# Score products of batches 1 to 3 on 128 rows throughout, and weighted sums with their 128-column products first

## The chip, the cores and the metric

The kernel runs on one core of one Trainium2 chip. The core has TensorE (PE in the profile; PEld is its weight load), VectorE (DVE), ScalarE (ACT), GpSimd (POOL) and SyncE (SP), each with its own instruction queue that is worked in order, and DMA queues that are fed from SP and ACT. The metric is the device time of one execution in microseconds, as the median of several runs.

## The reference

Attention with rotary positions, 4 batches of 8 heads, 576 positions, head size 64, followed by a two-layer MLP on all 2304 tokens. Everything is float32 on the outside.

```python
def rotate(x):
    x1, x2 = (x[..., :half], x[..., half:])
    return np.concatenate([x1 * cos - x2 * sin, x1 * sin + x2 * cos], axis=-1)
q_rot, k_rot = (rotate(q), rotate(k))
scores = scale * np.matmul(q_rot, k_rot.transpose(0, 1, 3, 2))
scores = scores - np.max(scores, axis=-1, keepdims=True)
attn = np.exp(scores)
attn = attn / (np.sum(attn, axis=-1, keepdims=True) + 1e-09)
x = np.matmul(attn, v)            # then (batch * position, 8 * 64)

h = x @ w_in                      # 512 -> 2048
sp = np.where(h > 20.0, h, np.log1p(np.exp(np.minimum(h, 20.0))))
out = (h * np.tanh(sp)) @ w_out   # 2048 -> 512
```

## The kernel before

The kernel works on pairs of heads: `P` counts 16 of them, four for each batch. A pair's positions are cut into four tiles of 128 queries for each head and one tail tile that holds the last 64 queries of both heads. Every such tile is one step: score products on TensorE into a PSUM tile `psc` (two buffers), maximum on VectorE (L520), exponential with its sum on ScalarE (L522), the reciprocal, and then the weights as a high and a low float16 part `ew` (L536 or L538 for the high one, L542 on VectorE for the low one). A DMA transposes `ew` into `et`. `av` makes the weighted sums: for each pair two of them, over 256 and 320 queries, into the PSUM tile `po`.

To keep accuracy, numbers are split into a high part that TensorE's fast float32 form holds exactly and a low rest. In batch 0 (`P < NP`) a score product is three passes over 64 rows. In batches 1 to 3 a product for one head is two passes, each of two matmuls of 288 columns (L495):

- the first has 128 rows. Its weights `xa` (or `xb` for the second head) hold the high part of q in the rows of the head and q's low part in the other 64 rows; the moving operand `y[:, h]` holds the high part of k twice;
- the second has only the head's own 64 rows: the high part of q times `kl`, the low part of k. `kl` has 128 rows, 64 for each head of the pair.

The tail product of a pair (`scores_tail`) has three passes, all of 128 rows: the two heads' high parts and, for the low part, `xdiag`, which holds the two heads' tail columns of q as a block diagonal, times `kl`. `xdiag` is filled by two copies on ScalarE for each pair (L412).

`kl` is made in `prep_k` by one subtraction on GpSimd with 128 rows and 576 columns (L437), from the rotated k (`raw`, L379 to L382 on GpSimd) and its high part. The high part is copied into `y` by four DMAs (L446). The tile `raw` of k is free for the next pair's load (L373, mostly issued from ScalarE's queue) when the subtraction and those copies are done.

A weighted sum of batches 1 to 3 has three passes: V high with weights high, V low with weights high, V high with weights low. A pass is one matmul with 128 weight columns (L666, the chunk that holds the end of both heads) and four pairs of matmuls with 64 weight columns (L669 and L670, one head each). The three passes are planned as two operations, of two passes and of one.

All other TensorE work is the MLP: L912 makes hidden columns into `ph`, L943 makes the output into `pp` or `po`, always in groups of 12 matmuls with 128 rows and 128 columns. The MLP of one batch is spread among the attention steps of the next.

The order of all this is not written by hand. `Plan.op` records every operation with the engines that may do it and a cost in ns. `Plan.order` plays them through with these costs and priorities and so decides the order of issue on each engine; the costs are hand-set (a score product has 2n x 228 ns for n passes, a weighted sum 17.4 matmul costs). On the chip every engine follows its order strictly.

Of the kernel before, what the change touches and what calls it, by code (L numbers as in the profile page):

```python
# [10 lines left out]
F32 = mybir.dt.float32  # L11
# [258 lines left out]
def attention_mish_mlp(ctx: ExitStack, tc: tile.TileContext, qk, v, vflat, rope, ident_in, w_in, w_out, outT):  # L270
# [14 lines left out]
    def sbuf(shape, dt, tag, bufs=1):  # L285
        return plan.tile(sb, shape, dt, tag, bufs)
# [15 lines left out]
    xq = [fixed((128, 1408), F32R, f"xq{r}") for r in range(2)]  # L302
    for t in (cs, ident, ones, cells, w1, w2, *xt, *xq):
        t()
# [91 lines left out]
    def prep_q(P):  # L396
# [4 lines left out]
        def view(a):  # L401
# [6 lines left out]
           w=parts(o, LO), r=parts(o, HI) + (parts(t, LO) if first else []))  # L408
        for x, p, k in ((xdiag[P % 2], 1, HI), (xlow[P % 2], 0, LO))[:2 if first else 1]:
            for h, a in ((0, 512), (1, 0)):  # L410
                d = slice(64 * h, 64 * h + 64)
                op((ACT, act_ns(64), lambda d=d, a=a, x=x, p=p: nc.scalar.activation(  # L412
                    x()[d, d], view(p)[d, a:a + 64], AF.Copy)), w=[(x, h)], r=parts(o, k))
# [15 lines left out]
    def prep_k(P):  # L429
        t = rope_turn(P, 1)  # L430
        y = sbuf((128, 2, S), F32R, "y", 2)
        first = P < NP
        hi = y if first else t
        kl = y if first else sbuf((128, S), F32R, "kl", 2)

        def low(e):
            e.tensor_tensor(out=kl()[:, 0] if first else kl(), in0=t()[:, 0], in1=hi()[:, 1], op=ALU.subtract)  # L437

        op((ACT, act_ns(S), lambda: nc.scalar.activation(
            hi()[:, 1] if first else hi()[:, 1].bitcast(F32R), t()[:, 0], AF.Copy)), w=parts(hi, HI), r=parts(t, LO))  # L440
        st["K", P] = y, kl
        if not first:
            for h in range(2):
                own = slice(64 * h, 64 * h + 64)
                for r in range(2):
                    load("xy", dma_ns(64 * S * 4, 625), lambda dma, h=h, r=r, own=own: dma(  # L446
                        y()[64 * r:64 * r + 64, h].bitcast(F32), t()[own, 1]), w=[(y, (h, r))], r=parts(t, HI))
        op([(POOL, pool_ns(S), lambda: low(nc.gpsimd)), (DVE, dve_ns(S), lambda: low(nc.vector))][:2 if first else KLW],
           w=parts(kl, LO) if first else [kl], r=parts(hi, HI) + parts(t, LO))

# [20 lines left out]
    def scores(pt, P, h, t):  # L471
        own = slice(64 * h, 64 * h + 64)
        y, kl = st["K", P]
        if P < NP:
            Q = xqs[P]
            q = slice(128 * t + 64 * h, 128 * t + 64 * h + 128)
            need = parts(Q, HI + LO) + parts(y, HI + LO)

            def terms():
                return [(Q()[own, i, q], y()[own, j]) for i, j in ((1, 1), (0, 1), (1, 0))]  # L480
        else:
            x = (xa, xb)[h][P % 2]
            q = slice(128 * (t + h), 128 * (t + h) + 128)
            need = [(x, k) for k in range(3)] + [(y, (h, 0)), (y, (h, 1)), kl]

            def terms():
                return [(x()[:, q], y()[:, h]), (x()[own, q], kl()[own])]

        product(pt, need, terms, 3 if P < NP else 2)

    def product(pt, need, terms, n):
# [4 lines left out]

        op((PE, 2 * n * 228, fn), w=[pt], r=need)

    def scores_tail(pt, P):
        d = xdiag[P % 2]  # L500
        y, kl = st["K", P]
        if P < NP:
            low = xlow[P % 2]
            need = [(low, 0), (low, 1)] + parts(y, HI + LO)

            def terms():
                return [(d(), y()[:, 1]), (low(), y()[:, 1]), (d(), y()[:, 0])]
        else:
            a, b = xa[P % 2], xb[P % 2]
            need = [(z, k) for z in (a, b) for k in range(3)] + [(y, (h, r)) for h in range(2) for r in range(2)] + [kl]  # L510

            def terms():
                return [(a()[:, 512:640], y()[:, 0]), (b()[:, 0:128], y()[:, 1]), (d(), kl())]

        product(pt, need + [(d, 0), (d, 1)], terms, 3)

# [131 lines left out]
    def av(P, k):  # L648
# [13 lines left out]

        def fn(passes):
            for vi, ei in passes:
                et = ET()[:, 9 * ei:9 * ei + 9]
                nc.tensor.matmul(po()[:, :n], V()[:, vi, 4, :], et[:, 4, :], start=vi == 0 and ei == 0, stop=False)  # L666
                for c in range(4):
                    last = ei == 1 and c == 3
                    nc.tensor.matmul(po()[0:64, :n], V()[:, vi, c, 0:64], et[:, c, :], start=False, stop=last)  # L669
# [5 lines left out]
        else:  # L675
            op((PE, 5.8 * pe_ns(2, n), lambda: fn([(0, 0), (1, 0)])), w=[po], r=[(V, 0), (V, 1)] + [(ET, x) for x in need])
            op((PE, 5.8 * pe_ns(1, n), lambda: fn([(0, 1)])), w=[po], r=[(V, 0)] + [(ET, x) for x in need])
        if p == 0 and k == 0:
# [357 lines left out]
    for t in xq:  # L1036
        nc.vector.memset(t()[:, 1152:1408].bitcast(F32), 0.0)
    program()
    with tc.manual_schedule():
# [62 lines left out]
```

## Time and profile before

| | us |
|---|---|
| median of 3 runs | 772.73 |
| lowest and highest run | 768.99 and 781.5 |
| span of the profiled execution, first to last instruction (its own time is not listed apart) | 760.5 |
| PE busy | 676.6 (89% of the span) |
| PEld busy | 493.0 (65%) |
| DVE busy | 484.8 (64%) |
| ACT busy | 401.8 (53%) |
| POOL busy | 304.9 (40%) |

The profile is one execution on the chip. It lists for each engine and line how long the instructions ran, and what ended the idle time before them (the releaser). "Issue" as a releaser means that the profile shows nothing that the engine waited for. Matmuls are pipelined, so what one costs is read from the distance between starts in the timeline rather than from its duration. A form like "64*128 64x288" means weights of 64 rows and 128 columns, and a moving operand of 64 rows and 288 columns. PEclk is the clock that TensorE was granted, as a share of 2.4 GHz.

### The profile page before, as it was taken

To read this page: it belongs to the slowest core of one execution; us is meant where nothing else is said; L and a number is where in the kernel's file an instruction comes from. 1 tells how busy PE (TensorE), PEld (TensorE's weight loads), DVE (VectorE), ACT (ScalarE), POOL (GpSimd) and SP (SyncE) were. 2 spreads that over 40 slices of the span, in tenths; PEclk is the share of its full clock that TensorE was granted. 3 is DMA by queue.
4 is the path that set the end of the run, shared out by engine and by line. 5 is a ranking of instruction groups with operands and counts; after the bars stand their busy time and mean duration, and the time that the engine had idled before them with its cause. 6 is when DMAs were issued, how large, how long until landed. Compare 5 with 4: busy or idle time off the path is not lost. (4 is left out here: it accounts for less than half of the span.)

```text
span 760.5 us, 12953 instructions
## 1 busy us (share of the span) xinstructions
PE 676.6 (89%) x4904; PEld 493.0 (65%) x4904; DVE 484.8 (64%) x873; ACT 401.8 (53%) x828; POOL 304.9 (40%) x268
## 2 busy tenths in 40 slices
PE   1968689786899889997899879988999999999998
PEld 1646566554675557765676567655777776777776
DVE  6899999879768857756367666737466637120110
ACT  3766667666565555645455446625554655242331
POOL 4488865649624736226333653335513101000000
PEclk9966868895999989998999999996999999999999
DMA  9942526266726991497728770766346605300000
GB/s 365 371 135 77 170 80 170 90 157 154 192 51 134 236 225 49 111 173 173 183 50 219 168 174 13 165 172 155 102 87 154 134 1 118 64 9 16 9 9 31
DMA packets 167213, 97.83 MB, mean 129 GB/s; under 512 B 130800, under 2 KB 151408, under 8 KB 167024
## 3 DMA queue, kind: packets, MB, share of 16 engines
q1 hardware_dynamic: 152784, 71.26, 39.3%
q10 hardware_dynamic: 14368, 25.76, 11.1%
q8 instruction: 38, 0.62, 0.3%
q14 instruction: 23, 0.19, 0.1%
HBM read 46.27 MB, written 4.72 MB: 67 GB/s over the span
## 5 line engine op out<-in xcount | busy, mean ns | idle before, releaser
L912 PE MATMUL ph<-xt,w 128*128 128x288 f16 x1344 | 178.9, 292 | 14.3 <-ACT mh L917 14.1
L912 PEld LDWEIGHTS <-w 128*128 128x128 f16 x1536 | 152.0, 100 | 58.8 <-issue 18.0
L943 PE MATMUL pp<-g,w 128*128 128x288 f16 x1344 | 184.3, 291 | 1.1 <-ACT ot L951 1.1
L943 PEld LDWEIGHTS <-w 128*128 128x128 f16 x1536 | 147.1, 99 | 49.0 <-issue 11.5
L522 ACT ACTIVATE e<-psc,mx 128x576 f32<-128x576 f32 x144 | 105.8, 737 | 83.3 <-DVE mx L520 75.7
L495 PE MATMUL psc<-y,xq 128*128 128x288 f32 (+1 forms) x456 | 109.7, 365 | 40.4 <-ACT e L522 25.4
L536 POOL TENSOR_SCALAR ew<-e,rs 128x576 f16<-128x576 f32 x62 | 48.7, 788 | 188.4 <-DVE rs L532 121.9
L542 DVE SCALAR_TENSOR_TENSOR ew<-e,rs,ew 128x576 f16<-128x576 f32 x108 | 106.1, 1009 | 28.4 <-POOL ew L536 16.0
L379 POOL TENSOR_TENSOR raw<-raw,cs 128x576 f32<-128x576 f32 x62 | 98.0, 1596 | 59.4 <-DMA raw<-in_qk 39.6
L929 DVE SCALAR_TENSOR_TENSOR g<-mh,cells,g 128x576 f16<-128x576 f32 x64 | 61.4, 961 | 90.0 <-ACT g L926 89.5
L520 DVE TENSOR_REDUCE mx<-psc 128x1 f32<-128x576 f32 x144 | 106.6, 747 | 18.3 <-PE psc L495 17.5
L495 PEld LDWEIGHTS psc<-y,xq 128*128 128x128 f32 (+1 forms) x456 | 75.1, 221 | 60.7 <-ACT e L522 31.3
L917 ACT ACTIVATE mh<-ph,cells 128x288 f32<-128x288 f32 x112 | 54.6, 497 | 86.3 <-PE ph L912 72.6
L382 POOL TENSOR_TENSOR raw<-raw 128x288 f32<-128x288 f32 x60 | 64.0, 1084 | 0.0
L495 PE MATMUL psc<-kl,xq 64*128 64x288 f32 (+1 forms) x216 | 58.6, 353 | 0.0
L758 POOL TENSOR_TENSOR w<-mr,w 128x512 f16<-128x512 f32 x32 | 41.1, 1291 | 36.9 <-ACT w L756 24.8
L669 PE MATMUL po<-et,v 128*64 128x256 f16 (+1 forms) x288 | 51.9, 306 | 0.0
L670 PE MATMUL po<-et,v 128*64 128x256 f16 (+1 forms) x288 | 51.8, 305 | 0.0
L538 ACT ACTIVATE ew<-e,rs 128x576 f16<-128x576 f32 x46 | 35.3, 771 | 25.6 <-DMA et<-ew 9.8
L495 PEld LDWEIGHTS psc<-kl,xq 64*128 64x128 f32 (+1 forms) x216 | 34.1, 196 | 16.4 <-issue 16.0
L927 DVE TENSOR_SCALAR g<-mh,cells 128x576 f16<-128x576 f32 x21 | 15.5, 738 | 43.6 <-ACT mh L917 22.8
L530 DVE TENSOR_SCALAR sm<-sm 128x2 f32<-128x2 f32 (+1 forms) x80 | 26.9, 336 | 22.2 <-ACT e L522 21.8
(111 smaller groups left out, 809.7 us busy)
## 6 DMA issues: line engine op xcount, KB each, us to landing
raw<-in_qk ACTq DMA_DIRECT2D x22, 576.0 KB, 4.9
xq<-raw SPq DMA_DIRECT2D x48, 144.0 KB, 2.7
y<-raw SPq DMA_DIRECT2D x48, 144.0 KB, 3.6
raw<-in_qk SPq DMA_DIRECT2D x10, 576.0 KB, 4.6
out_dram<-ot ACTq DMA_DIRECT2D x32, 144.0 KB, 1.9
g<-in_w_in SPq DMA_DIRECT2D x4, 1024.0 KB, 7.6
w<-in_w_in SPq DMA_DIRECT2D x4, 1024.0 KB, 15.2
stg<-in_v ACTq DMA_DIRECT2D x11, 320.0 KB, 3.8
```

The lines of the kernel that those rows point to most:

```text
L379: e.tensor_tensor(out=t()[:, :, s], in0=t()[:, :, s], in1=cs()[:, :, s], op=ALU.mult)
L382: e.tensor_tensor(out=t()[:, 0, s], in0=t()[:, 0, s], in1=t()[:, 1, s], op=ALU.add)
L495: nc.tensor.matmul(pt()[:, c, :HS], x, z[:, c * HS:(c + 1) * HS], start=a == 0, stop=a == n - 1)
L520: op((DVE, dve_ns(S), lambda: nc.vector.tensor_reduce(m(), pt()[:, :, :HS], axis=AX.XY, op=ALU.max, negate=True)), w=[m], r=[pt])
L522: op((ACT, act_ns(S, psum=True, ptr=2), lambda: nc.scalar.activation(e().rearrange("p (c s) -> p c s", c=2), pt()[:, :, :HS], AF.Exp, bias ...
L542: op((DVE, dve_ns(S) + 61, lambda: nc.vector.scalar_tensor_tensor(out=w()[:, c], in0=e(), scalar=r()[:, h:h + 1], in1=w()[:, hc], op0=ALU. ...
L669: nc.tensor.matmul(po()[0:64, :n], V()[:, vi, c, 0:64], et[:, c, :], start=False, stop=last)
L670: nc.tensor.matmul(po()[64:128, :n], V()[:, vi, c, 64:128], et[:, 5 + c, :], start=False, stop=last)
L912: nc.tensor.matmul(hp(), w1()[:, wi, cc, f:f + 128], x()[:, xi, cc, hf * HS:(hf + 1) * HS], start=cc == 0 and a == 0, stop=cc == NCC - 1 a ...
L917: op((ACT, act_ns(HS, psum=True, ptr=1), lambda j=j, hp=hp: nc.scalar.activation(hn()[:, j], hp(), AF.Mish, scale=uh())), w=[(hn, j)], r=[ ...
L929: op((DVE, dve_ns(S) + 61, lambda: nc.vector.scalar_tensor_tensor(out=g()[:, 1, f], in0=hn(), scalar=f32(gs), in1=g()[:, 0, f], op0=ALU.mu ...
L943: nc.tensor.matmul(pp()[:, :HS], w2e[e]()[:, wi, f], g()[:, gi, f % 8, :], start=f == 0 and a == 0, stop=f == NF - 1 and a == 2)
```

## The change

Four things are changed.

1. The low part of k is kept in two fixed tiles `klz` of 128 rows, two heads and 576 columns. They are set to zero once at the start, on GpSimd. For each pair, GpSimd writes the low part of head h into the 64 rows of that head only, in two subtractions of 64 rows instead of one of 128. A score product's second pass then uses all 128 rows of q's tile and of `kl[:, h]`; the rows of q's low part meet zeros.
2. The tail has four passes, the high and the low part of k for each head. `xdiag` is no longer used in batches 1 to 3 and its two copies are left out there.
3. A weighted sum is one planned operation; its three 128-column matmuls come first, then the 24 matmuls with 64 columns.
4. The costs for the planner follow: 2n x 132 ns for a score product, in batch 0 too, and 15 matmul costs plus 220 ns for a weighted sum. The scratch memory for DMAs is set to 1024 bytes.

```diff
+    klz = [fixed((128, 2, S), F32R, f"kl{r}", planned=False) for r in range(2)]
...
-        for x, p, k in ((xdiag[P % 2], 1, HI), (xlow[P % 2], 0, LO))[:2 if first else 1]:
+        for x, p, k in ((xdiag[P % 2], 1, HI), (xlow[P % 2], 0, LO))[:2 if first else 0]:
...
-        kl = y if first else sbuf((128, S), F32R, "kl", 2)
-
-        def low(e):
-            e.tensor_tensor(out=kl()[:, 0] if first else kl(), in0=t()[:, 0], in1=hi()[:, 1], op=ALU.subtract)
+        kl = y if first else klz[P % 2]
+
+        def low(e, rows=slice(0, 128), h=0):
+            e.tensor_tensor(out=kl()[rows, h], in0=t()[rows, 0], in1=hi()[rows, 1], op=ALU.subtract)
...
+        for h in range(0 if first else 2):
+            rows = slice(64 * h, 64 * h + 64)
+            op([(POOL, pool_ns(S), lambda rows=rows, h=h: low(nc.gpsimd, rows, h)),
+                (DVE, dve_ns(S), lambda rows=rows, h=h: low(nc.vector, rows, h))][:KLW],
+               w=[(kl, h)], r=parts(hi, HI) + parts(t, LO))
...
-                return [(x()[:, q], y()[:, h]), (x()[own, q], kl()[own])]
+                return [(x()[:, q], y()[:, h]), (x()[:, q], kl()[:, h])]
...
-        op((PE, 2 * n * 228, fn), w=[pt], r=need)
+        op((PE, 2 * n * 132, fn), w=[pt], r=need)
...
-                return [(a()[:, 512:640], y()[:, 0]), (b()[:, 0:128], y()[:, 1]), (d(), kl())]
-
-        product(pt, need + [(d, 0), (d, 1)], terms, 3)
+                ends = a()[:, 512:640], b()[:, 0:128]
+                return [(ends[h], z[:, h]) for z in (y(), kl()) for h in range(2)]
+
+        product(pt, need, terms, 3 if P < NP else 4)
...
-        def fn(passes):
-            for vi, ei in passes:
-                et = ET()[:, 9 * ei:9 * ei + 9]
-                nc.tensor.matmul(po()[:, :n], V()[:, vi, 4, :], et[:, 4, :], start=vi == 0 and ei == 0, stop=False)
+        def fn():
+            passes = [(vi, ET()[:, 9 * ei:9 * ei + 9]) for vi, ei in ((0, 0), (1, 0), (0, 1))]
+            for i, (vi, et) in enumerate(passes):
+                nc.tensor.matmul(po()[:, :n], V()[:, vi, 4, :], et[:, 4, :], start=i == 0, stop=False)
+            for i, (vi, et) in enumerate(passes):
                 for c in range(4):
...
-            op((PE, 5.8 * pe_ns(2, n), lambda: fn([(0, 0), (1, 0)])), w=[po], r=[(V, 0), (V, 1)] + [(ET, x) for x in need])
-            op((PE, 5.8 * pe_ns(1, n), lambda: fn([(0, 1)])), w=[po], r=[(V, 0)] + [(ET, x) for x in need])
+            op((PE, 5 * pe_ns(3, n) + 220, fn), w=[po], r=[(V, 0), (V, 1)] + [(ET, x) for x in need])
...
+    for t in klz:
+        nc.gpsimd.memset(t().bitcast(F32), 0.0)
```

## Rows read from the trace of the kernel before

**Rows 1.** Windows: stretch, then busy us of each engine (instructions), clock, DMA.

```profile
156.00:280.00 124.00, 105.10 (x696) 71.91 (x697) 99.39 (x170) 70.81 (x148) 70.46 (x56) 0.88 0.71 166
280.00:521.00 241.00, 221.56 (x1683) 159.09 (x1680) 153.00 (x258) 124.20 (x251) 100.27 (x86) 0.98 0.59 138
521.00:645.00 124.00, 123.88 (x931) 90.64 (x932) 74.38 (x126) 70.68 (x140) 30.68 (x31) 0.96 0.49 109
```

**Rows 2.** Waits of PE from 280 to 521 us: total us, times, longest.

```profile
PE psc L495 <- ACT e L522: 8.8, 3, 5.0
PE ph L912 <- ACT mh L917: 8.4, 7, 2.0
```

**Rows 3.** The chain that ended last: start us, us, what.

```profile
497.75 0.77 DVE mx L520
...
521.12 3.04 PE psc L495 x10
...
528.27 19.48 PE ph L912 x144
...
600.40 17.66 PE ph L912 x144
```

**Rows 4.** Timeline of PE: start us, us, instruction, tile, form, count.

```profile
402.14 0.31 PE L666 MATMUL po<-et,v 128*128 128x320 f16 x1
402.38 0.32 PE L669 MATMUL po<-et,v 128*64 128x320 f16 x1
...
402.81 0.30 PE L669 MATMUL po<-et,v 128*64 128x320 f16 x1
...
403.05 0.53 PE L495 MATMUL psc<-y,xq 128*128 128x288 f32 x2
403.51 0.53 PE L495 MATMUL psc<-kl,xq 64*128 64x288 f32 x2
403.97 1.64 PE L943 MATMUL pp<-g,w 128*128 128x288 f16 x12
405.36 0.78 PE L495 MATMUL psc<-y,xq 128*128 128x288 f32 x4
405.98 0.42 PE L495 MATMUL psc<-kl,xq 128*128 128x288 f32 x2
406.24 1.64 PE L943 MATMUL pp<-g,w 128*128 128x288 f16 x12
```

**Rows 5.** Groups by line and form: busy us, mean ns, idle before and releasers.

```profile
L495 PEld LDWEIGHTS psc<-kl,xq 64*128 64x128 f32 x192 | 29.7, 194 | 16.4 <-issue 16.0 <-POOL kl L437 0.2 <-POOL raw L379 0.2
```

**Rows 6.** Three lines' own views: duration in ns (min/median/max), first and last start.

```profile
L437 POOL TENSOR_TENSOR kl<-raw x12: 1400/1411/2008, 124.8 to 574.4; 128x576 fp32r<-128x576 f32 x12
L412 ACT ACTIVATE xq<-raw x24: 239/252/257, 125.2 to 575.2; 64x64 fp32r<-64x64 f32 x24
L542 DVE SCALAR_TENSOR_TENSOR ew<-e,rs,ew x108: 799/818/2009, 162.2 to 647.7; 128x576 f16<-128x576 f32 x108
```

**Rows 7.** Timeline of all engines from 439 to 452 us.

```profile
439.12 1.95 DVE L542 SCALAR_TENSOR_TENSOR ew<-e,rs,ew 128x576 f16<-128x576 f32 x1
...
440.42 1.92 POOL L437 TENSOR_TENSOR kl<-raw 128x576 fp32r<-128x576 f32 x1
...
450.80 0.33 ACTq L373 DMA_DIRECT2D raw<-in_qk  x1
...
451.74 1.51 PE L912 MATMUL ph<-xt,w 128*128 128x288 f16 x11 [1.96 <-ACT mh L917]
```

**Rows 8.** Timeline of the start: GpSimd's first rotation.

```profile
6.08 3.54 POOL L379 TENSOR_TENSOR raw<-raw,cs 128x576 f32<-128x576 f32 x2 [5.64 <-DMA raw<-in_qk]
```

**Rows 9.** Groups by form, 156 to 280 us, then 280 to 521 us.

```profile
L495 PE MATMUL psc<-kl,xq 64*128 64x288 f32 x48 | 13.3, 359 | 0.0
L495 PE MATMUL psc<-kl,xq 64*128 64x288 f32 x94 | 25.8, 355 | 0.0
```

**Rows 10.** Windows, as rows 1: behind the chain's part without TensorE.

```profile
515.00:532.00 17.00, 15.10 (x67) 9.66 (x68) 13.84 (x18) 9.53 (x19) 8.99 (x8) 0.61 0.61 144
```

More of the change, by code (lines that the diff above doesn't have):

```diff
@@ L302, in attention_mish_mlp @@
     xq = [fixed((128, 1408), F32R, f"xq{r}") for r in range(2)]
-    for t in (cs, ident, ones, cells, w1, w2, *xt, *xq):
+    klz = [fixed((128, 2, S), F32R, f"kl{r}", planned=False) for r in range(2)]
+    for t in (cs, ident, ones, cells, w1, w2, *xt, *xq, *klz):
         t()
@@ L447, in prep_k @@
                         y()[64 * r:64 * r + 64, h].bitcast(F32), t()[own, 1]), w=[(y, (h, r))], r=parts(t, HI))
-        op([(POOL, pool_ns(S), lambda: low(nc.gpsimd)), (DVE, dve_ns(S), lambda: low(nc.vector))][:2 if first else KLW],
-           w=parts(kl, LO) if first else [kl], r=parts(hi, HI) + parts(t, LO))
+        if first:
+            op([(POOL, pool_ns(S), lambda: low(nc.gpsimd)), (DVE, dve_ns(S), lambda: low(nc.vector))],
+               w=parts(kl, LO), r=parts(hi, HI) + parts(t, LO))
+        for h in range(0 if first else 2):
[3 more added lines that the diff above has]
+               w=[(kl, h)], r=parts(hi, HI) + parts(t, LO))
     def load_v(P):
@@ L483, in scores @@
             q = slice(128 * (t + h), 128 * (t + h) + 128)
-            need = [(x, k) for k in range(3)] + [(y, (h, 0)), (y, (h, 1)), kl]
+            need = [(x, k) for k in range(3)] + [(y, (h, 0)), (y, (h, 1)), (kl, h)]
             def terms():
-                return [(x()[:, q], y()[:, h]), (x()[own, q], kl()[own])]
+                return [(x()[:, q], y()[:, h]), (x()[:, q], kl()[:, h])]
         product(pt, need, terms, 3 if P < NP else 2)
@@ L495, in fn @@
                     nc.tensor.matmul(pt()[:, c, :HS], x, z[:, c * HS:(c + 1) * HS], start=a == 0, stop=a == n - 1)
-        op((PE, 2 * n * 228, fn), w=[pt], r=need)
+        op((PE, 2 * n * 132, fn), w=[pt], r=need)
     def scores_tail(pt, P):
-        d = xdiag[P % 2]
         y, kl = st["K", P]
         if P < NP:
-            low = xlow[P % 2]
-            need = [(low, 0), (low, 1)] + parts(y, HI + LO)
+            d, low = xdiag[P % 2], xlow[P % 2]
+            need = [(z, h) for z in (d, low) for h in range(2)] + parts(y, HI + LO)
             def terms():
@@ L509, in scores_tail @@
             a, b = xa[P % 2], xb[P % 2]
-            need = [(z, k) for z in (a, b) for k in range(3)] + [(y, (h, r)) for h in range(2) for r in range(2)] + [kl]
+            need = [(z, k) for z in (a, b) for k in range(3)] + [(y, (h, r)) for h in range(2) for r in range(2)] + [(kl, 0), (kl, 1)]
             def terms():
-                return [(a()[:, 512:640], y()[:, 0]), (b()[:, 0:128], y()[:, 1]), (d(), kl())]
-        product(pt, need + [(d, 0), (d, 1)], terms, 3)
+                ends = a()[:, 512:640], b()[:, 0:128]
+                return [(ends[h], z[:, h]) for z in (y(), kl()) for h in range(2)]
+        product(pt, need, terms, 3 if P < NP else 4)
     def max_exp(pt, h, sm):
@@ L661, in exact_fn @@
                 nc.tensor.matmul(po()[64:128, :n], V()[:, c, 64:128], ET()[:, 5 + c, :], start=False, stop=c == 3)
-        def fn(passes):
-            for vi, ei in passes:
-                et = ET()[:, 9 * ei:9 * ei + 9]
-                nc.tensor.matmul(po()[:, :n], V()[:, vi, 4, :], et[:, 4, :], start=vi == 0 and ei == 0, stop=False)
+        def fn():
[3 more added lines that the diff above has]
+            for i, (vi, et) in enumerate(passes):
                 for c in range(4):
-                    last = ei == 1 and c == 3
+                    last = i == 2 and c == 3
                     nc.tensor.matmul(po()[0:64, :n], V()[:, vi, c, 0:64], et[:, c, :], start=False, stop=last)
@@ L1090 @@
     laid = _layout(**inputs)
-    nc = _bacc.Bacc("TRN2", target_bir_lowering=False, num_devices=1)
+    nc = _bacc.Bacc("TRN2", target_bir_lowering=False, num_devices=1, dynamic_dma_scratch_size=1024)
     arrays, args = {}, []
```

## The prediction

> **What bounds the kernel now.** I first cut the part that the change touches, batches 1 to 3, into three stretches of the windows view [rows 1]. From 521 to 645 us TensorE is busy for 123.88 of 124 us. From 280 to 521 us it is busy for 221.56 of 241 us. From 156 to 280 us it is busy for 105.10 of 124 us, and VectorE, with 99.39 us, comes close. Then the waits of TensorE: in the middle stretch it waits 8.8 us for exponentials to free a bank and 8.4 us for activations of the MLP [rows 2]. Last the chain that ended last [rows 3]: from 521.12 us on it lies nearly all on TensorE (its pieces at 521.12, 528.27 and 600.40 us stand for the rest). Before that it has one long part without TensorE, 497.75 to 521.12 us, which begins with a maximum on VectorE; weight subtractions there and exponentials on ScalarE follow each other. So a microsecond taken off TensorE is worth a microsecond in the last stretch, a good part of one in the middle, and less at the start of batch 1.
>
> **Scores: what the change removes.** The timeline of TensorE at full clock shows one step by step [rows 4]. A score product of batches 1 to 3 is two 128-row matmuls, starting at 403.05 us, and two 64-row matmuls, starting at 403.51 us; the next work starts at 403.97 us. That is 0.92 us for four matmuls of 288 columns. The tail product a little later has six matmuls of the same size and type, all with 128 rows: 405.36 to 405.98 us for the first four and 406.24 us for the end, 0.88 us for six, 0.147 us each. What is left over in the 0.92 us is the change from 128 to 64 rows and back. The weight loads show the same thing from the other side: before the 64-row ones their engine stood idle for 16.0 us without a releaser [rows 5]. Zeros in the other half of k's low part cost the matmul nothing, as the tail's rows show. In the new form a product is four matmuls of 128 rows. I take 4 x 0.147 = 0.59 us. The bounds are 0.62 us, which the first four of the tail took, and 0.52 us, twice its last pair's 0.26 us. Saved per product: 0.33 us (0.30 to 0.40). There are 192 of the 64-row matmuls [rows 5], two for each product, so 96 products: 31.7 us (28.8 to 38.4).
>
> **The tail: what it adds.** Each of the 12 tails (one for each pair of heads) goes from three passes to four, two matmuls more: 2 x 0.147 = 0.29 us, 3.5 us in all (3.1 with 0.13 us each).
>
> **Weighted sums: the order.** One pass is a 128-column matmul and four pairs of 64-column halves. In the pass at 402.14 us the first pair comes 0.24 us later; three steps from pair to pair take 0.43 us, 0.14 us each; and the step out of the last pair, from 402.81 to 403.05 us, takes 0.24 us again [rows 4]. A change of column mode thus costs about 0.10 us. A sum has three passes, so six changes; the new order has two. Saved: 4 x 0.10 = 0.40 us, in 24 sums (two for each pair of heads): 9.6 us. Merging the two planned operations into one changes no instruction; it takes away the point at which another product can be put in, as the product at 403.05 us is put behind a pass. I cost that at nothing, because from 280 us on TensorE is busy for 95% of the time and has other work in its queue; without that cover a product comes later by up to one pass, 0.91 us (402.14 to 403.05 us).
>
> **Sum on TensorE.** 31.7 + 9.6 - 3.5 = 37.8 us less work (34.9 to 44.9 us with the bounds of the products and tails), worked at the full clock; stretches at 1.2 GHz would give somewhat more.
>
> **The other engines.** ScalarE loses the 24 copies of the diagonal blocks, 0.25 us each [rows 6], 6 us over 490 us; it is not the bound, so I count nothing. GpSimd makes the low part of k in two operations of 64 rows instead of one of 128. No row shows a 64-row subtraction there. One of 128 rows takes 1.41 us at the median and 2.01 us at most [rows 6]. A half can cost half of it, so that nothing is added, or all of it, so that 12 x 1.41 = 17 us are added (24 us with the longest). I take the whole, because the half has the same operation and the same number of columns as that row. The Trainium skill, GPSIMD Engine Reference, section 2.1 Instruction dispatch, speaks against the change here: each core serves its own 16 partitions of every instruction, so an instruction on half the partitions leaves cores idle and gets no shorter. By it the sum on GpSimd is 17 us more, otherwise 0; no run so far shows which.
>
> What hides these 17 us: GpSimd is busy for 201 of the 489 us [rows 1]. Its result is needed only at the next pair's first product. The second half also holds the raw tile of k longer, for whose release a later load waits on ScalarE's queue. In the pair at 440 us the subtraction ended at 442.34 us, but that load was let go only at 450.80 us, by the copies of k's high part [rows 7]. A half that ends 1.4 to 2.0 us later still ends some 6 us before that. Without this cover each pair would lose those 1.4 to 2.0 us.
>
> The clearing of the two new low tiles is put in front of GpSimd's first rotation, which starts at 6.08 us after 5.64 us of waiting for its load [rows 8]. The tiles have 2 x 1152 columns; at the price of the 576-column subtraction with two inputs, 1.41 us, that is 5.6 us at most, and a fill should be cheaper. I take it as hidden; without that cover it would be up to 5.6 us. The smaller DMA scratch moves no instruction of the trace: 0.
>
> **From the sum to the end.** The 64-row matmuls number 48 and 94 in the first two stretches [rows 9], so 50 of the 192 are left for the last: 24, 47 and 25 products. Sharing 37.8 us out that way gives 9.4, 18.5 and 9.9 us. In the last stretch I count all of it: 9.9 us. In the middle one TensorE is busy for 92% of the time, but 23.4 us of the chain there go by without it in one part, and more waits could open: I take 0.7, 13.0 us. In the first one VectorE is busy almost as long as TensorE and TensorE already stands idle for 19 us: I take 0.4, 3.8 us. Together 26.7 us. The profiled execution's span of 760.5 us becomes 733.8 us. The median of the three runs is 772.73 us, 12.2 us above that span; with the same distance the kernel takes **746 us**. The choice with most weight is the share of the middle stretch; from 0.4 to 1 it moves the result by 11 us.
>
> The planner also gets new costs (2n x 132 ns for 2n x 228 ns, for batch 0 too) and will put the instructions of all engines in another order. No view of before prices that; it is the main reason for the width of the range.
>
> **Rivals.**
> *VectorE takes the gain.* The subtraction of the weights takes 0.82 us at the median but up to 2.01 us [rows 6], and at 439.12 us it took 1.95 us while GpSimd worked on two inputs [rows 7]. If each of the 12 added halves lengthens one such operation by 1.13 us on the path, 13.6 us go: 746 + 13.6 = 760 us, no measurable change. For it: VectorE starts the part of the chain from 497.75 to 521.12 us. Against it: there are 108 such subtractions, nine for each added half, and VectorE is idle for a third of the 489 us. The Trainium skill, GPSIMD Engine Reference, section 1 Specifications, says that the two engines share their SBUF interface and that VectorE's instructions with two SBUF inputs contend there; the trace agrees with the 1.95 us.
>
> *The whole saving arrives.* If today's waits only wait for TensorE's earlier work, all 37.8 us count: 735 us; with the upper bounds 728 us. For it: activations of the MLP and exponentials both start from what TensorE wrote.
>
> *The clock falls.* From 515 to 532 us, behind the part of the chain without TensorE, the granted clock was 0.61, so partly 1.2 GHz [rows 10]; the 144 MLP matmuls that start at 528.27 us took 19.48 us, the 144 at 600.40 us took 17.66 us [rows 3]: 1.8 us lost. If TensorE waits more often, four more such places cost 7 us: 753 us. The Trainium skill, TensorE: Matmul & The Clock Gate, Part 1, calls the throttled clock the default that activity releases; the drop behind the waits agrees.
>
> *Slower: the new order blocks ScalarE's queue.* A load of raw q or k issued there holds everything behind it until its buffer is free. The one let go at 450.80 us made an MLP activation late and with it TensorE by 1.96 us [rows 7]; with 1.8 us of slower clock behind it a hold costs up to 3.8 us. Three new holds bring the kernel within 2% of before (11.1 us); eleven make it slower by over 2%, 26.7 + 15.5 = 42 us, some 790 us. Against it: that is nearly one more in every pair of batches 1 to 3.
>
> *No saving in the products*, because their loads fail to hide: only 9.6 - 3.5 = 6 us, 767 us. The tail's 0.147 us speaks against it.
>
> **Chances.** Some 2% is what a measurement of this kernel can tell from no change, so faster means below 757.3 us and slower above 788.2 us. The forecast, 740 to 757 us, with the clock's case in it: 0.58. The whole saving, 725 to 740 us: 0.20. VectorE takes it, or a few holds do: 0.14. No saving in the products: 0.02. Blocked queue, slower: 0.06. That gives faster 0.78, within 2% 0.16, slower 0.06. The range from 727 to 765 us leaves out the slow case and the ends of the others.
>
> **What would show it.** Right: score products of 0.5 to 0.6 us, no 64-row form in batches 1 to 3 and no idle time of its loads; L666's matmuls in runs of three, 0.11 to 0.14 us apart; TensorE's busy time down by 30 us or more; GpSimd with 24 subtractions of 1.4 us or more. Wrong: waits of TensorE for exponentials from 280 to 521 us that grow by more than 10 us, weight subtractions on VectorE much longer than now, longer holds of ScalarE's queue by loads, or a lower clock after 280 us.

## The result and the profile after

| | before | changed |
|---|---|---|
| median, us (4 runs each) | 773.82 | 738.65 |
| lowest and highest, us | 768.99, 781.5 | 737.41, 740.41 |
| ratio of the changed kernel | | 0.957 (95% interval 0.951 to 0.963) |
| span of the profiled execution, us | 760.5 | 735.6 |

The changed kernel is faster by 35 us between the medians and by 33 us by the ratio, within the stated range of 727 to 765 us and 7 us below the predicted 746 us. Runs of the kernel before, and of most kernels in its order, spread over 10 to 24 us, so a median below is that of all runs, a ratio to the kernel before is that of the fast runs alone (within 1.5% of the fastest of their kernel), and differences of medians under some 6 us are read as none.

TensorE's busy time fell by 27.2 us, from 676.6 us, at nearly the same mean granted clock (0.928 before, 0.930 after). The prediction had named 30 us or more as a sign of being right; this sign was narrowly missed. The line of the page (busy us, share of the span, instructions):

```profile
PE 649.4 (88%) x4928; PEld 500.7 (68%) x4928; DVE 479.1 (65%) x876; ACT 397.3 (54%) x806; POOL 321.1 (44%) x277
```

TensorE's timeline of the changed kernel answers to [rows 4]:

```profile
404.77 0.52 PE L502 MATMUL psc<-y,xq 128*128 128x288 f32 x2
405.12 0.43 PE L502 MATMUL psc<-kl,xq 128*128 128x288 f32 x2
405.39 0.42 PE L502 MATMUL psc<-y,xq 128*128 128x288 f32 x2
405.66 0.43 PE L502 MATMUL psc<-kl,xq 128*128 128x288 f32 x2
405.93 1.65 PE L950 MATMUL pp<-g,w 128*128 128x288 f16 x12
407.41 0.57 PE L673 MATMUL po<-et,v 128*128 128x320 f16 x3
407.91 0.32 PE L677 MATMUL po<-et,v 128*64 128x320 f16 x1
...
409.43 0.30 PE L677 MATMUL po<-et,v 128*64 128x320 f16 x1
```

The second product runs from 405.39 to 405.93 us: 0.54 us instead of 0.92 us. The first, which stands behind a group of the MLP, takes 0.62 us, from 404.77 to 405.39 us. The whole timeline of batches 1 to 3 has this pattern: products without a wait inside take 0.54 us at the median behind another product and 0.63 us behind other work. The mean of the 79 that can be read off is 0.63 us, where the kernel before has 0.92 us in both places. So a product saves 0.29 us in the mean, some 28 us for 96 products. In the weighted sum three 128-column matmuls and one change of mode take 0.50 us, and the eleven steps from the first pair to the last take 1.52 us, 0.14 us each.

The weight loads of the second pass answer to [rows 5], with no idle time without a releaser; beside them stand the clearing of the low tiles, and, from the line's own view, the halves on GpSimd, which answer to the first of [rows 6] (count: ns min/median/max):

```profile
L502 PEld LDWEIGHTS psc<-kl,xq 128*128 128x128 f32 x240 | 40.2, 200 | 0.0
...
L1046 POOL MEMSET kl<- 128x1152 f32 x2 | 2.1, 1059 | 0.3 <-POOLq L1100 0.3
...
L438 POOL TENSOR_TENSOR kl<-raw x24: 1393/1502/1996, 136.1 to 557.7; 64x576 fp32r<-64x576 f32 x24
```

So every step of the change did on its engine about what the prediction said. Where the time came off is another matter. The copy of a weighted sum to `xt` on ScalarE marks the progress. These are, in each kernel, the last copies of batches 0, 1, 2 and 3; first before, then the changed kernel (start us, us, instruction):

```profile
162.22 0.56 ACT L692 ACTIVATE xt<-ew,cells 128x320 f16<-128x320 f32 x1
...
338.49 0.44 ACT L692 ACTIVATE xt<-po 128x320 f16<-128x320 f32 x1 [3.66 <-DMA xq<-raw]
...
504.21 0.44 ACT L692 ACTIVATE xt<-po 128x320 f16<-128x320 f32 x1 [4.48 <-DMA xq<-raw]
...
658.68 0.44 ACT L692 ACTIVATE xt<-po 128x320 f16<-128x320 f32 x1 [4.33 <-PE po L670]
```

```profile
166.62 0.56 ACT L699 ACTIVATE xt<-ew,cells 128x320 f16<-128x320 f32 x1 [2.93 <-DVE ew L696]
...
329.57 0.44 ACT L699 ACTIVATE xt<-po 128x320 f16<-128x320 f32 x1 [0.39 <-DMA xq<-raw]
...
485.61 0.44 ACT L699 ACTIVATE xt<-po 128x320 f16<-128x320 f32 x1 [2.03 <-DMA y<-raw]
...
635.32 0.44 ACT L699 ACTIVATE xt<-po 128x320 f16<-128x320 f32 x1 [5.35 <-PE po L678]
```

Batch 1 became shorter by 13.3 us (176.3 to 163.0), batch 2 by 9.7 us (165.7 to 156.0), batch 3 by 4.8 us (154.5 to 149.7). I had forecast the opposite: least at the start and all of it at the end. Each batch has the same 32 products, so cheaper products alone don't explain this pattern. The windows of the changed kernel, cut like [rows 1] but at its own places, show that TensorE is no longer without gaps in the last stretch (111.73 of 118 us, before 123.88 of 124 us):

```profile
156.00:280.00 124.00, 103.44 (x772) 79.39 (x771) 107.09 (x199) 74.57 (x150) 79.85 (x64) 0.90 0.70 172
280.00:502.00 222.00, 198.01 (x1629) 154.77 (x1627) 147.48 (x255) 118.41 (x237) 109.73 (x94) 0.98 0.68 154
502.00:620.00 118.00, 111.73 (x925) 89.57 (x925) 70.33 (x119) 67.10 (x130) 34.17 (x34) 0.97 0.50 105
```

Two explanations compete: the cheaper instructions, as I had argued, or the other order that the planner made from its new costs, which I had priced at nothing.

### The profile page after: what moved, and what is told of

Same layout as the page of the kernel before. It is cut to its first block, busy times and chain, and to the rows that moved or that the text cites. A ratio compares the mean times of both kernels' runs of the same rounds, so it can differ in the third digit from the quotient of the medians.

```text
span 735.6 us, 12977 instructions
## 1 busy us (share of the span) xinstructions
PE 649.4 (88%) x4928; PEld 500.7 (68%) x4928; DVE 479.1 (65%) x876; ACT 397.3 (54%) x806; POOL 321.1 (44%) x277
## 5 line engine op out<-in xcount | busy, mean ns | idle before, releaser
L919 PE MATMUL ph<-xt,w 128*128 128x288 f16 x1344 | 174.2, 288 | 17.1 <-ACT mh L924 16.9
L529 ACT ACTIVATE e<-psc,mx 128x576 f32<-128x576 f32 x144 | 105.7, 737 | 76.5 <-DVE mx L527 51.9
L549 DVE SCALAR_TENSOR_TENSOR ew<-e,rs,ew 128x576 f16<-128x576 f32 x108 | 109.7, 1044 | 25.7 <-ACT ew L545 13.5
L380 POOL TENSOR_TENSOR raw<-raw,cs 128x576 f32<-128x576 f32 x62 | 96.5, 1572 | 60.2 <-DMA raw<-in_qk 47.2
L936 DVE SCALAR_TENSOR_TENSOR g<-mh,cells,g 128x576 f16<-128x576 f32 x64 | 64.2, 1006 | 86.1 <-ACT g L933 85.5
L502 PEld LDWEIGHTS psc<-y,xq 128*128 128x128 f32 (+1 forms) x456 | 78.0, 228 | 60.0 <-ACT e L529 37.2
L765 POOL TENSOR_TENSOR w<-mr,w 128x512 f16<-128x512 f32 x32 | 39.2, 1236 | 51.1 <-ACT w L763 39.5
L502 PE MATMUL psc<-kl,xq 128*128 128x288 f32 x240 | 51.7, 307 | 0.0
L438 POOL TENSOR_TENSOR kl<-raw 64x576 fp32r<-64x576 f32 x24 | 38.4, 1601 | 10.1 <-ACT raw L440 6.4
L678 PE MATMUL po<-et,v 128*64 128x256 f16 (+1 forms) x288 | 42.3, 299 | 0.2 <-DMA et<-ew 0.2
L677 PE MATMUL po<-et,v 128*64 128x256 f16 (+1 forms) x288 | 42.4, 299 | 0.0
L502 PEld LDWEIGHTS psc<-kl,xq 128*128 128x128 f32 x240 | 40.2, 200 | 0.0
```

The source lines that it names most:

```text
L380: e.tensor_tensor(out=t()[:, :, s], in0=t()[:, :, s], in1=cs()[:, :, s], op=ALU.mult)
L502: nc.tensor.matmul(pt()[:, c, :HS], x, z[:, c * HS:(c + 1) * HS], start=a == 0, stop=a == n - 1)
L529: op((ACT, act_ns(S, psum=True, ptr=2), lambda: nc.scalar.activation(e().rearrange("p (c s) -> p c s", c=2), pt()[:, :, :HS], AF.Exp, bias ...
L549: op((DVE, dve_ns(S) + 61, lambda: nc.vector.scalar_tensor_tensor(out=w()[:, c], in0=e(), scalar=r()[:, h:h + 1], in1=w()[:, hc], op0=ALU. ...
L919: nc.tensor.matmul(hp(), w1()[:, wi, cc, f:f + 128], x()[:, xi, cc, hf * HS:(hf + 1) * HS], start=cc == 0 and a == 0, stop=cc == NCC - 1 a ...
L936: op((DVE, dve_ns(S) + 61, lambda: nc.vector.scalar_tensor_tensor(out=g()[:, 1, f], in0=hn(), scalar=f32(gs), in1=g()[:, 0, f], op0=ALU.mu ...
```

## Experiments

**The parts undone in the changed kernel's order.** The second pass on 64 rows again, with every engine's order of issue as in the changed kernel:

```diff
-                return [(x()[:, q], y()[:, h]), (x()[:, q], kl()[:, h])]
+                return [(x()[:, q], y()[:, h]), (x()[own, q], kl()[own, h])]
```

> The changed kernel with one thing undone: the second pass of a score product uses only the head's own 64 rows of q and of the low part of k again. Everything else is the changed kernel's, the planned order of all engines too. Theory (the change of row mode costs TensorE time, and most of it reaches the end): a product takes 0.9 us again instead of 0.53, 96 x 0.37 = 36 us more on TensorE, of which 0.65 to 1 reaches the end, so 762 to 775 us; idle time without a releaser before the 64-row weight loads comes back, about 16 us. Rival (the new order of the planner brought the gain): the order is the same, so it stays within 6 us of the changed kernel's 738.7 us.

Measured: 749.33 us median (746.55 to 754.38). The timeline shows the old price again:

```profile
410.14 0.52 PE L502 MATMUL psc<-y,xq 128*128 128x288 f32 x2
410.59 0.53 PE L502 MATMUL psc<-kl,xq 64*128 64x288 f32 x2
411.05 0.53 PE L502 MATMUL psc<-y,xq 128*128 128x288 f32 x2
```

and so do the weight loads:

```profile
L502 PEld LDWEIGHTS psc<-kl,xq 64*128 64x128 f32 x192 | 29.3, 191 | 16.3 <-issue 16.3
```

From 410.14 to 411.05 us a product takes 0.91 us, and the idle time without a releaser is back. The 36 us that I had expected are too many, because they take every product of the changed kernel at 0.53 us. Mean against mean (0.91 and 0.63 us) TensorE has 96 x 0.28 = 27 us more to do, and the busy times agree: 676.1 against 649.4 us, at granted clocks of 0.929 and 0.930. But against the 738.65 and 735.92 us of the changed kernel only 11 to 13 us arrive at the end, 0.4 to 0.5 of it. Both theories miss: the row mode counts, but most of the gain remains without it. The marks on ScalarE say where it counts:

```profile
166.44 0.56 ACT L699 ACTIVATE xt<-ew,cells 128x320 f16<-128x320 f32 x1 [2.10 <-DVE ew L696]
...
334.39 0.44 ACT L699 ACTIVATE xt<-po 128x320 f16<-128x320 f32 x1 [0.22 <-PE po L678]
...
493.97 0.44 ACT L699 ACTIVATE xt<-po 128x320 f16<-128x320 f32 x1 [2.33 <-DMA y<-raw]
...
652.31 0.44 ACT L699 ACTIVATE xt<-po 128x320 f16<-128x320 f32 x1 [5.35 <-PE po L678]
```

Batches 1, 2 and 3 take 168.0, 159.6 and 158.3 us, so in one profile against one profile the row mode is worth 5.0, 3.5 and 8.6 us of the 9 us that 32 products cost. (This profiled execution is 5 us slower than its median, so the three are some us too large in sum.)

The sum pass by pass again, still one planned operation with the same cost:

```diff
             for i, (vi, et) in enumerate(passes):
                 nc.tensor.matmul(po()[:, :n], V()[:, vi, 4, :], et[:, 4, :], start=i == 0, stop=False)
-            for i, (vi, et) in enumerate(passes):
                 for c in range(4):
```

> The changed kernel with one thing undone: in a weighted sum each pass does its 128-column matmul and then its halves, as before the change; it stays one planned operation with the same cost, so the order of all engines is the changed kernel's. Theory (a change of column mode costs 0.10 us): four changes more in each of 24 sums, 9.6 us more on TensorE, of which 6 to 10 us reach the end: 745 to 749 us. Rival (the order inside the sum doesn't matter, the row mode alone does): 738 to 741 us.

Measured: 737.00 us (735.12 to 739.30), no different from the changed kernel. On the engine the changes of mode are back, 0.23 us into the first pair and 0.23 us out of the last:

```profile
406.71 0.30 PE L673 MATMUL po<-et,v 128*128 128x320 f16 x1
406.94 0.32 PE L676 MATMUL po<-et,v 128*64 128x320 f16 x1
...
407.37 0.30 PE L676 MATMUL po<-et,v 128*64 128x320 f16 x1
...
407.60 0.31 PE L673 MATMUL po<-et,v 128*128 128x320 f16 x1
```

That is 0.10 us for each change, 24 x 4 x 0.10 = 10 us more work. TensorE does this work: it was busy for 649.2 us at a mean granted clock of 0.949, and a second profile of the changed kernel, at the same clock, has 10.5 us less:

```profile
PE 638.7 (87%) x4928; PEld 492.5 (67%) x4928; DVE 484.8 (66%) x876; ACT 397.0 (54%) x806; POOL 318.4 (43%) x277
```

But nothing of it can be seen at the end, as the rival said. The order inside the sums is not a part of the gain.

**The planner's costs.** The changed kernel's instructions with the costs of before:

```diff
-        op((PE, 2 * n * 132, fn), w=[pt], r=need)
+        op((PE, 2 * min(n, 3) * 228, fn), w=[pt], r=need)
...
-            op((PE, 5 * pe_ns(3, n) + 220, fn)
+            op((PE, 5.8 * pe_ns(3, n), fn)
```

> The changed kernel's instructions, but the planner is given the costs of before: 228 ns for each matmul of a score product (six of them for a tail) and 5.8 matmul costs for each pass of a weighted sum. So only the order of issue differs from the changed kernel. Theory (the gain comes from cheaper instructions; the order moves the time by some us either way): 730 to 748 us. Rival (the better costs of the planner bring a good part of the gain): 750 to 765 us.

Measured: 769.63 us, ratio to before 1.002 (0.996 to 1.009). All the cheaper instructions are in, and nothing is gained.

```profile
PE 647.6 (84%) x4928; PEld 500.3 (65%) x4928; DVE 473.3 (61%) x867; ACT 400.2 (52%) x812; POOL 319.3 (41%) x280
```

TensorE is busy for 647.6 us of a span of 771.1 us: it stands idle for 123.5 us, against 83.9 us before. My theory (730 to 748 us) fell, and the rival's 750 to 765 us was not enough.

The other side, the kernel before with the new costs and no instruction changed:

```diff
-        op((PE, 2 * n * 228, fn), w=[pt], r=need)
+        op((PE, 2 * n * 132, fn), w=[pt], r=need)
```

(and the weighted sum's two operations at the new price).

> The kernel before with the planner's new costs alone (132 ns for each matmul of a score product, 15 matmul costs and 220 ns for a weighted sum, shared out over its two operations); no instruction is changed, only their order. Theory (the order is worth some us either way): 765 to 782 us, within 2% of before. Rival (the order brings the gain): 745 to 757 us. Third possibility, that the costs which are now too low for the old instructions spoil the order: over 789 us.

Measured: 755.52 us (754.34 to 756.71), ratio 0.987 (0.980 to 0.994), in the rival's range. By the ratio that is 10 us; beside the medians of the kernel before, 773.82 and 776.66 us, it is 18 to 21 us. So the order alone brings 10 us or more with the old instructions.

```profile
PE 683.5 (91%) x4904; PEld 496.7 (66%) x4904; DVE 474.1 (63%) x880; ACT 401.3 (53%) x826; POOL 298.7 (40%) x263
```

TensorE works no less (683.5 us), but of the span of 752.5 us it is idle for only 69.0 us.

Which costs make this order? The new cost for batch 0 alone and for batches 1 to 3 alone, again with the old instructions:

```diff
-        op((PE, 2 * n * 228, fn), w=[pt], r=need)
+        op((PE, 2 * n * (132 if n == 3 and exact0 else 228), fn), w=[pt], r=need)
```

> The kernel before with no instruction changed; the planner's new cost of 132 ns only for the score products of batch 0, so only the order differs. If the gain of the new costs (some 10 to 18 us with the old instructions) comes from batch 0, whose products were priced too high: 750 to 760 us, with the gain inside batch 1's stretch. If it comes from batches 1 to 3: 764 to 776 us. If any change of cost shuffles the order by chance, it may lie anywhere within 15 us of before.

```diff
-        op((PE, 2 * n * 228, fn), w=[pt], r=need)
+        op((PE, 2 * n * (228 if exact0 else 132), fn), w=[pt], r=need)
```

> The kernel before with no instruction changed; the planner's new costs only for batches 1 to 3 (132 ns for each matmul of their score products, the new price of a weighted sum), batch 0 as before. If the gain of the order comes from batches 1 to 3: 750 to 760 us. If it comes from batch 0: 764 to 776 us. If both this and the run with batch 0 alone show neither, the gain is that of one order among many, and not of a price that is now right.

Measured: 776.31 us, ratio 1.004 (0.996 to 1.011), and 771.06 us, ratio 0.995 (0.989 to 1.001). Neither alone gives the gain of both. So the order's gain can't be put down to one price that is now right; with the old instructions it looks like one order among many. With the new instructions a cost between the two was tried:

```diff
-        op((PE, 2 * n * 132, fn), w=[pt], r=need)
+        op((PE, 2 * n * 160, fn), w=[pt], r=need)
```

> The changed kernel's instructions, with 160 ns instead of 132 ns as the planner's cost of each matmul of a score product; only the order differs. If the gain of the order comes from a cost that is right (the products measure 0.13 us for each matmul) and fades as it goes wrong: 742 to 755 us. If every small change of cost gives another order by chance: anywhere from 735 to 770 us, also below the changed kernel.

Measured: 741.72 us (739.79 to 749.10). This other order is nearly as good as the changed kernel's. A product of 0.54 to 0.63 us is 135 to 158 ns for each matmul, so 132 and 160 ns lie at the two ends of the real price. Together with 769.63 us at 228 ns that speaks for costs near the real ones, but the run at 228 ns has another cost for the sums too, and three orders don't settle it.

**Why the old order gives nothing back.** The planner was shown exactly the operations and costs of before, so all engines keep their old order, and only the instructions behind the score products changed:

```diff
+            for h in range(2):
+                rows = slice(64 * h, 64 * h + 64)
+                e.tensor_tensor(out=kl()[rows, h], in0=t()[rows, 0], in1=hi()[rows, 1], op=ALU.subtract)
...
-                return [(x()[:, q], y()[:, h]), (x()[own, q], kl()[own])]
+                return [(x()[:, q], y()[:, h]), (x()[:, q], kl()[:, h])]
...
-        op((PE, 2 * n * 228, fn), w=[pt], r=need)
+        op((PE, 2 * min(n, 3) * 228, fn), w=[pt], r=need)
```

> The kernel before, in exactly its own order of issue on all engines (the planner sees the costs and the operations of before), but with the new score instructions: 128 rows in every pass of batches 1 to 3, four passes in the tail, two 64-row subtractions on GpSimd one right behind the other, cleared low tiles. The two copies for the block diagonal stay, unused; weighted sums are as before. Theory A (the saved TensorE time counts by itself, and the order of the run with old costs was merely a poor one): 740 to 752 us. Theory B (the old order leaves the saving no place: TensorE comes sooner to products that wait for a bank or for the MLP's activations): 757 to 772 us, and the waits of TensorE for exponentials and activations grow by 20 us or more.

Measured: 771.92 us (767.61 to 777.23), ratio 1.006 (1.001 to 1.010): no gain at all, in the range of theory B, though a product takes 0.65 us in the mean instead of 0.92 us, some 25 us less for 96. The same two waits of TensorE in the whole of the kernel before (total us, times, longest), then here:

```profile
PE psc L495 <- ACT e L522: 25.4, 13, 5.0
PE ph L912 <- ACT mh L917: 14.1, 10, 3.0
```

```profile
PE psc L501 <- ACT e L529: 40.1, 23, 5.8
PE ph L919 <- ACT mh L924: 20.3, 11, 4.6
```

They grew by 20.9 us, as theory B said. One of the places, in the stretch where TensorE had been busy without a gap before [rows 1]:

```profile
537.89 5.33 SPq L634 DMA_TRANSPOSE et<-ew  x1
...
543.29 1.02 SPq L452 DMA_DIRECT2D y<-raw  x1
...
548.92 0.34 ACTq L374 DMA_DIRECT2D raw<-in_qk  x1
549.36 0.89 ACT L924 ACTIVATE mh<-ph,cells 128x288 f32<-128x288 f32 x2 [5.66 <-DMA y<-raw]
...
549.91 2.32 PE L919 MATMUL ph<-xt,w 128*128 128x288 f16 x9 [4.62 <-ACT mh L924]
```

The last copy of k's high part is issued from SyncE only at 543.29 us. ScalarE's queue stands before the load of the next raw tile until that copy has landed; the MLP activation behind the load is 5.66 us late, and TensorE waits 4.62 us. This is the hold of [rows 7], in a place that had none. In front of the copy on SyncE's queue stood a transpose of 5.33 us, which ended right before it. In the kernel before, the transpose in front of the same copy took 1.81 us:

```profile
531.01 1.81 SPq L627 DMA_TRANSPOSE et<-ew  x1
532.86 0.59 SPq L446 DMA_DIRECT2D y<-raw  x1
```

The sum of these holds over the kernel, first before, then here (total us, times, longest):

```profile
ACT mh L917 <- DMA y<-raw: 6.0, 2, 3.1
```

```profile
ACT mh L924 <- DMA y<-raw: 17.2, 4, 5.7
```

Two more runs take this apart, both in the old order. One has 128 rows in the second pass but no halves: GpSimd, the tail and all else are as before. (The other 64 rows then hold the other head's low part instead of zeros, so a wrong small term is added.)

```diff
-                return [(x()[:, q], y()[:, h]), (x()[own, q], kl()[own])]
+                return [(x()[:, q], y()[:, h]), (x()[:, q], kl())]
```

> The kernel before in exactly its own order, with one thing changed: the second pass of a score product uses 128 rows, over the undivided low part of k, so that GpSimd's work, the tail and everything else are those of before. (The other half of the rows is not zero, so a wrong small term is added.) TensorE gets its 0.37 us for each product, GpSimd has no second half. If the 17 us of GpSimd's second halves ate the saving in the run with the old order: 740 to 752 us. If the old order itself leaves the saving no place: 760 to 773 us, like that run, with longer waits of TensorE for exponentials and activations.

Measured: 763.03 us (760.05 to 769.03), ratio 0.981 (0.975 to 0.988); before had 776.86 us beside it. So without the halves some 14 us arrive of the 25 us that the products save here, and with them nothing: the halves, with the tail's two extra matmuls for each pair, cost some 9 us between the medians. (The two runs were not timed side by side, but their ratios' intervals lie apart.) The time lies in the range of the second forecast, and the two waits of TensorE are longer than before, as it said; but the run is not like the one with halves. The halves ate a part and the order kept the rest. The hold on ScalarE is smaller, and at the place above the transpose in front of the copy still took 4.23 us, so the halves alone did not make it long:

```profile
PE psc L495 <- ACT e L522: 37.3, 23, 5.1
PE ph L912 <- ACT mh L917: 17.7, 8, 4.7
ACT mh L917 <- DMA y<-raw: 12.2, 3, 5.2
...
539.24 4.23 SPq L627 DMA_TRANSPOSE et<-ew  x1
```

The other run keeps the halves and takes the hold away: the loads of raw q and k are issued from SyncE, at the same place of the order.

```diff
-        op((ACT if on_act else SP, ns, lambda: fn((nc.scalar if on_act else nc.sync).dma_start)), w=w, r=r)
+        op((ACT if on_act else SP, ns, lambda: fn((nc.scalar if on_act and kind != "qk" else nc.sync).dma_start)), w=w, r=r)
```

> The run with the old order and the new score instructions (771.9 us), with one thing changed: the loads of raw q and k of the later pairs are issued from SyncE's queue instead of ScalarE's, at the same place of the order. So ScalarE's activations are no longer queued behind a load that waits for the copies out of the raw tile. If those holds of ScalarE (17.2 us of waits of MLP activations for these copies in the old order, 6.0 us in the kernel before) are what ate the saving: 750 to 762 us. If the bound is the preparation of the next pair itself, or SyncE's transposes now queue behind the loads: 765 to 785 us.

Measured: 762.95 us (756.73 to 770.00), ratio 0.977 (0.970 to 0.985), just above the range of the first forecast and 9 us less than the median with the loads on ScalarE, which was again not timed side by side. The waits of TensorE are shorter:

```profile
PE psc L501 <- ACT e L529: 35.0, 24, 4.2
PE ph L919 <- ACT mh L924: 14.7, 9, 3.2
```

So ScalarE's queue, held by a load, is one place where the saving of TensorE went in the old order, some 9 us of it.

The same edit in the changed kernel, and the changed kernel again:

> The changed kernel in its own order, with the loads of raw q and k of the later pairs issued from SyncE's queue instead of ScalarE's. It tells whether the holds of ScalarE cost the changed kernel time too (9.3 us of waits of activations and 9.8 us of exponentials for the copies out of the raw tile). If they do: 722 to 733 us, faster than both kernels. If not, or if the transposes on SyncE's queue are held instead: 734 to 750 us.

> The changed kernel, unaltered, on the same chip as the three others, so that their times can be set beside it: 735 to 742 us.

Measured: 736.34 us (732.44 to 740.96), and 735.92 us (734.59 to 739.97) for the changed kernel. The holds cost the new order nothing that can be measured, and this version doesn't beat the changed kernel.

**The balance.** Span, busy time and idle time of TensorE from the profiles, the mean granted clock of the profiled execution, and the median of the runs:

| kernel | order | median | span | busy | idle | clock |
|---|---|---|---|---|---|---|
| before | old | 773.82 | 760.5 | 676.6 | 83.9 | 0.928 |
| 128 rows, no halves | old | 763.03 | 763.1 | 659.1 | 104.0 | 0.922 |
| score instructions of the change | old | 771.92 | 770.2 | 659.2 | 111.0 | 0.925 |
| the same, loads from SyncE | old | 762.95 | 758.5 | 657.7 | 100.8 | 0.928 |
| before, new costs | new costs | 755.52 | 752.5 | 683.5 | 69.0 | 0.927 |
| changed, 64 rows | changed | 749.33 | 752.6 | 676.1 | 76.5 | 0.929 |
| changed, sums by pass | changed | 737.00 | 737.4 | 649.2 | 88.2 | 0.949 |
| changed | changed | 738.65 | 735.6 | 649.4 | 86.2 | 0.930 |
| changed, again | changed | 735.92 | 738.2 | 638.7 | 99.5 | 0.949 |

Two profiles of the changed kernel differ by 10.7 us of busy time, so only rows of like clock are set side by side. Cheaper products turn into idle time, in whole or in part: 17 us less busy becomes 27 us more idle in the old order, 27 us less busy becomes 10 us more idle in the new one.

Of the 35 us of the result, 11 to 13 us go when the 128 rows are undone, and nothing that shows when the sums' order is undone. What is left with the row mode undone is 24 us between the medians, or 16 us by that run's ratio to before, 0.980. It comes from all that this run keeps, and mainly from the order of issue: the new costs with the old instructions bring 10 us by the ratio and up to 21 us between medians, and the new instructions without the new costs bring nothing. The shares need not add up, since the same instructions are worth nothing to 14 us in the old order. The smaller DMA scratch was not run alone; the two runs that have it with the old costs (771.92 and 769.63 us) gain nothing.

## Why the prediction was right, and where it was not

The time came out in the range, but for reasons that were largely others, and that is luck. The forecast had 26.7 us from cheaper instructions and nothing from the order; undoing the instructions takes back 11 to 13 us, and most of the rest came with the order. The two errors nearly cancel.

- **Products, 0.59 us (0.52 to 0.62).** Nearly right: 0.54 us behind another product, 0.63 us behind other work, 0.63 us in the mean, just above the upper bound. I had taken the mean of six matmuls of the tail; its first four, 0.62 us behind an MLP group, were the nearer row. The saving on TensorE is some 28 us rather than 31.7 us.
- **Tail and sums on the engine.** Right: a tail's eight matmuls take 1.16 us (from 313.52 to 314.68 us in the changed kernel) instead of 0.88 us for six, a change of column mode costs 0.10 us with the passes mixed, and the three leading matmuls follow as forecast. The Trainium skill, TensorEngine Tiling, section Key Properties, says that changing the tiling mode drains TensorE; 16.3 us of idle loads with 64 rows and 0.0 us without agree.
- **GpSimd's halves, 17 us added.** Right, with 19 us: 1.50 us for 64 rows against 1.41 us for 128 at the median, 38.4 us for 24 against 19.2 us for 12. The Trainium skill, GPSIMD Engine Reference, section 2.1 Instruction dispatch, says that each core works on its own 16 partitions of an instruction. It follows that half the partitions save no time, and the trace agrees.
- **What hides them.** Wrong in the old order: some 9 us are lost with them and the longer tail. I named the tile's release and ScalarE's queue and read one pair where the copies came later by 6 us; elsewhere the hold grew. At the place shown the copy stood behind a long transpose on SyncE's queue; this was long without the halves too (4.23 us), and why is not shown. The path from the halves to the other holds is only argued. In the changed order taking the hold away gave nothing.
- **The clearing at the start.** Hidden, as said; two fills of 1.06 us instead of my bound of 5.6 us, and the first rotation starts at 6.17 us instead of 6.08 us.
- **From the sum to the end: 26.7 of 37.8 us.** This step failed. Of the row mode's 27 us some 0.4 to 0.5 arrive in the new order (11 to 13 us), and about half in the old order without halves (14 of 25 us). Of the sums' 10 us nothing arrives. The share of the last stretch was right for the products (8.6 of 9 us in one profile) and that of the first not far off (5.0 of 9 us, forecast 0.4); that of the middle, 0.7, was much too high (3.5 of 9 us). A stretch in which TensorE is busy for 92% of the time can have other chains just behind: a little less work on TensorE, and it waits longer for exponentials and for activations. In the old order that happened even in the last stretch, with 4.62 us in one place.
- **The planner's order, priced at nothing.** This was the largest error. I called it the main reason for the width of the range and gave it a rival only on the slow side. A rival in which the order itself gains was missing. It brings 10 us by the ratio and up to 21 us between medians with the old instructions, and without it the new instructions bring nothing (769.63 us).
- **Span to run, 12.2 us.** Mis-sized: the profiled execution of the changed kernel took 737.41 us with a span of 735.6 us, 1.8 us apart. The profiled execution of before was thus one of some 762 us, faster than all four timed runs of it. Span against span the change gives 24.9 us, median against median 35.2 us.
- **Rivals.** By its number, 735 us, the rival in which the whole saving arrives fits better than the forecast, but its mechanism fails: most of the saving does not arrive. VectorE did not take the gain: the weight subtraction has 0.82 us at the median before and after, and all 108 together went from 106.1 to 109.7 us, not up by 13.6 us. The clock did not fall: 0.90, 0.98 and 0.97 in the three stretches, before 0.88, 0.98 and 0.96. The blocked queue of ScalarE is real. It costs some 9 us where the order was not made for the new times; in the changed kernel its holds are longer than before too (activations and exponentials wait 19.1 us for the copies of k's high part, before 6.0 us), which was a sign of being wrong, but they cost nothing there that can be measured. TensorE's waits for exponentials in the middle stretch grew from 8.8 to 14.5 us, less than the 10 us more that was to speak against the forecast.

Open is what makes the new order better. Neither half of the new costs does it alone, and 160 ns gives nearly the same time as 132 ns.

## What to carry to other kernels

Where a program plans the order of issue from costs, a change of costs is a change of its own: time the old instructions in the new order and the new instructions in the old order before putting a gain down to either. A saving on an engine that is busy for 90% of the time need not arrive whole: here 11 to 13 us did of the 37 us of the products and sums, and nothing in the old order. After an engine gets faster, look for queues that issue both loads and compute work, since a load that waits for a buffer there holds the compute work behind it.

## What the runs showed of the hardware

A GpSimd subtraction on 64 rows took 1.50 us, no less than the 1.41 us on 128 rows. A fill of 128 x 1152 float32 values took 1.06 us there. 128-row float32 matmuls of 288 columns followed each other at 0.13 us although each has its own weight load of 0.2 us; behind float16 matmuls the first four took 0.62 us instead of 0.54 us. With 64-row ones in between the same four matmuls took 0.91 us in either place.
